# Packed attention and two feed-forward layers on one core: four conversions of w_in2 moved to the end of attention, w_out2's combinations kept as two split parts

## The chip, the cores and the metric

The kernel runs on one core of one Trainium2 chip. The metric is device time in microseconds (us) of one execution. The engines are TensorE (PE in the profile, its weight loads PEld), VectorE (DVE), ScalarE (ACT), GpSimd (POOL) and SyncE (SP). SP issues all DMAs here; sixteen DMA engines move the data.

## What is computed

The reference, cut to what matters:

```python
def sm_attn(qq, kk, vv):                       # softmax attention
    s = scale * qq @ kk.T; a = exp(s - max(s)); a = a / (sum(a) + 1e-09)
    return a @ vv
p_packed = sm_attn(p, k, v)                    # 8 batches, 8 heads, 32 packed queries, 576 keys, width 64
out = sm_attn(q, p_packed, p_packed)           # 576 queries over the 32 packed rows
x = out.transpose(0, 2, 1, 3).reshape(4608, 512)
h = x @ w_in                                   # first layer, 512 -> 2048
y = maximum(0.01 * h, h) @ w_out               # 2048 -> 512
h = y @ w_in2                                  # second layer, 512 -> 2048
result = (h * 1 / (1 + exp(-1.702 * h))) @ w_out2
```

The four weight matrices arrive as 64-bit floats, as pairs of 32-bit words, and have to be converted on the chip.

## The kernel before

**Stages.** There are four, one after the other on PE: attention with the first product h1 (`l1`, line 338; 256 steps, 32 for each of 8 batches), the product y (line 650, 6 blocks of 768 tokens), the product h of the second layer (line 684, 48 units) and the last product, called sum or d (line 762, 6 blocks).

**Seven products.** y, h and sum use Strassen's scheme: in a 2x2 splitting seven products of combinations stand in the place of eight. A y or sum block has 56 steps (7 products of 8 inner tiles), and the whole stage y 336; a unit of h has 7 steps, the whole stage 336 too.

**Split operands.** Each 32-bit operand is split into a high part (a ScalarE cast to fp32r) and a low part (a VectorE subtraction of the high part from the original, line 107); PE multiplies high by high, high by low and low by high. In y the moving operand `ba` is split so from `br`, two steps ahead (line 492 and line 107); `da` and `dr` are the same in the last stage. VectorE also forms the sums and differences of the `br` tiles (lines 480 to 486).

**Conversions.** `combine` converts one of 16 pieces of a weight matrix and forms its seven combinations: three loads into `raw` (512 KB in all), two ScalarE operations (lines 121 and 122, into the tiles `b` and `v`), a bit mask and a shift on VectorE (125 and 128), an integer addition on GpSimd (129), four VectorE subtractions (144 to 148), and a store of `b[:, 1:8]` to a scratch tensor in DRAM (448 KB). The tiles `raw`, `b` and `v` exist once each, so a conversion waits for the one before to be through with them. For w_out1 (`wo1`) the result is split on the spot: a cast and a subtraction into a tile `hl` of their own (lines 155 and 157), and two stores. For w_in2 (`wi2`) and w_out2 (`wo2`) the combinations are stored unsplit. Those of w_in2 are split as they are used in h (`wj`); those of w_out2 in `weights`: each of 14 weight tiles is loaded into its low half, and two times a ScalarE cast (line 459) and a VectorE subtraction follow, each on half of the tile, five tiles (`EARLY`) in stage h, nine in the first block of the last stage.

**What sets the order.** Everything is written out by hand: `at(step, ...)` puts a piece of work into an agenda, `side(step)` issues it between the matmuls of the steps, and each engine runs its instructions in that order. `pieces` spreads one conversion over steps; `combined(what, first, late)` starts one at each step s of `first` and does the rest at s+late, s+late+1, s+late+2, s+late+5 and so on. Before the change the w_in2 conversions begin in y at steps 26 and 44 of block 0, at 1, 19 and 38 of blocks 1 to 4, and at 1 and 19 of block 5; those of w_out2 in h every 15 steps, with late 10. In attention there are those of w_out1, every 11 steps from step 30 to 195, with late 8.

**Around the border of attention and y.** From step 212 on SP also loads the first weights of y (`wo_early`), and at step 248 the twelve first `br` tiles; it stores two h1 tiles of g after every four steps (line 347). The weights that are not early (`wo`) take memory that attention's tiles give back when their last stores have landed.

Of the kernel before, what the change touches and what calls it, by code (L numbers as in the profile page):

```python
# [9 lines left out]
F32 = mybir.dt.float32  # L10
# [11 lines left out]
P = 128  # L22
# [24 lines left out]
def packed_attention_moe_moe_kernel(tc, qT, kT, vm, vt, pT, w_in1, w_out1, w_in2, w_out2, out):  # L47
# [8 lines left out]
    wi2c, wo2c = (tc.dram_tile([NJ, P, 7, 256], F32, name=f"{n}_scratch") for n in ("wi2", "wo2"))  # L56
    wo1c = tc.dram_tile([NJ, P, 2, 7, 256], F32, name="wo1_scratch")
# [22 lines left out]
    with ExitStack() as ctx:  # L80
# [51 lines left out]
        def combine(name, source, scratch):  # L132
# [16 lines left out]
            if scratch is not wo1c:  # L149
                yield  # L150
                nc.sync.dma_start(place(name, scratch), b[:, 1:8])
                return
            yield
            h = pools["px"].tile([P, 2, 7, P], F32R, tag="hl", name=f"hl_{name}")
            nc.scalar.copy(h[:, 0], b[:, 1:8])
            yield
            nc.vector.tensor_sub(h[:, 1], b[:, 1:8], h[:, 0].bitcast(F32))
            yield
            for x in range(2):
                nc.sync.dma_start(place(name, scratch)[:, x], h[:, x].bitcast(F32))  # L160
# [5 lines left out]
        def combined(what, first, late):  # L166

            view, to = {"wo1": (w_out1_v, wo1c), "wi2": (w_in2_v, wi2c), "wo2": (w_out2_v, wo2c)}[what]
            for n, s in enumerate(first):
                j, u = divmod(n, 2)  # L170
                src = view[:, :, u, :, j, :] if what == "wi2" else view[:, :, j, :, u, :]
                pieces(combine(f"{what}_{j}_{u}", src, to), (s, *(s + late + k for k in (0, 1, 2, 5, 6, 7, 8, 9))))
# [258 lines left out]
        combined("wo1", range(30, 30 + 16 * 11, 11), 8)  # L431

# [3 lines left out]
        def weights(first, halves, i, fq, home, scratch, nm):  # L436
# [3 lines left out]
            def load():  # L440
                if n < EARLY:
                    if n == 0:
                        early[nm] = pools["A"].tile([P, 7 * 4 * HB], F32R, tag="A", name=f"{nm}_early")
                    t = early[nm][:, 2048 * n:2048 * n + 2048].rearrange("p (s f w) -> p s f w", s=2, f=4)
                else:
                    t = pools[home].tile([P, 2, 4, 256], F32R, tag=f"w{n}", name=f"{nm}_{p}_{fq}")
                wt[p, fq] = t
                for x in range(2):
                    if scratch is wo1c:
                        nc.sync.dma_start(t[:, x].bitcast(F32), scratch[4 * fq:4 * fq + 4, :, x, COMBO[p], :].rearrange("f p w -> p f w"))  # L450
                    elif x:
                        nc.sync.dma_start(t[:, 1].bitcast(F32), scratch[4 * fq:4 * fq + 4, :, COMBO[p], :].rearrange("f p w -> p f w"))
            at(first, load)
            if scratch is wo1c:
                return

            def half(k):
                hi, lo = (wt[p, fq][:, s, 2 * k:2 * k + 2, :] for s in range(2))
                nc.scalar.copy(hi, lo.bitcast(F32))
                return lo, lo.bitcast(F32), hi.bitcast(F32)  # L460
            for k, step in enumerate(halves):
                split(step, lambda k=k: half(k))
# [70 lines left out]
        def later_weights(home, scratch, nm):  # L533
            for n in range(EARLY, 14):
                i, fq = divmod(n, 2)
                weights(max(8 * (i - 2) + 2 * fq - 8, -2), (8 * i - 6 + 2 * fq, 8 * i - 5 + 2 * fq), i, fq, home(n), scratch, nm)


        for k in range(EARLY):
            s = 32 * (B - 2) + 20 + 8 * k  # L540
            weights(s, (s + 5, s + 7), k // 2, k % 2, None, wo1c, "wo1")
# [94 lines left out]
        combined("wi2", [26, 44] + [56 * blk + k for blk in range(1, 5) for k in (1, 19, 38)] + [281, 299], 14)  # L636
# [91 lines left out]
        for k in range(EARLY):  # L728
            s = 7 * (4 * NJ + 2 * k + 2)
            weights(s, (s + 8, s + 12), k // 2, k % 2, None, wo2c, "wo2")  # L730
# [81 lines left out]
```

## Time and profile before

| | us |
|---|---|
| median of 3 runs | 1481.79 (1481.16 to 1482.88) |
| the profiled execution, its own time | 1488.2 |
| its span, first to last instruction | 1486.4 |
| PE busy / PEld busy | 1417.2 / 1322.9 |
| VectorE busy | 1107.5 |
| ScalarE busy | 836.2 |
| GpSimd busy | 100.4 |
| data moved by DMA | 317.42 MB, 214 GB/s on average |

PE is busy for 95% of the span; the other engines are read where PE has to wait. A time in the rows below counts from the start of the span. A bracket behind a row is the idle time of its engine just before it, and what ended it.

### The profile page before, as it was taken

How to read it: one execution, taken by the hardware profiler on the slowest of the kernel's cores; microseconds unless marked ns; L12 is line 12 of the kernel's file. 1: busy time of each engine (PE TensorE's matmuls, PEld its weight loads, DVE VectorE, ACT ScalarE, POOL GpSimd, SP SyncE). 2: the span in 40 equal slices, each digit the busy share in tenths (PEclk: the TensorE clock that was granted, in tenths of full speed). 3: DMA queues.
4: the chain of work that ended last, by engine and by line, in shares of the span. 5: the costliest groups of instructions: out<-in, count | busy, mean ns of one | idle time of the engine just before them, and what ended most of it. 6: DMA issues, size and time to landing. Idle time of an engine off the chain costs nothing.

```text
span 1486.4 us, 27714 instructions
## 1 busy us (share of the span) xinstructions
PE 1417.2 (95%) x10400; PEld 1322.9 (89%) x10400; DVE 1107.5 (75%) x2068; ACT 836.2 (56%) x1791; POOL 100.4 (7%) x71
## 2 busy tenths in 40 slices
PE   6789999999979999999889999999999999999998
PEld 4567777778979999999789999999999999999998
DVE  5667777762859888888987887877648877777776
ACT  3656666665435545555656766666645655445443
POOL 1311110100001010110100010000000000000000
PEclk8889999999989999999999999999999999999999
DMA  9459999969993655635357786786768524515421
GB/s 365 159 194 318 308 325 307 335 212 337 325 301 118 212 187 164 223 105 197 120 184 249 250 282 238 244 276 204 242 216 276 170 88 148 181 54 170 129 85 43
DMA packets 228773, 317.42 MB, mean 214 GB/s; under 512 B 12576, under 2 KB 188704, under 8 KB 228640
## 3 DMA queue, kind: packets, MB, share of 16 engines
q1 hardware_dynamic: 228640, 315.67, 63.9%
q8 instruction: 81, 1.33, 0.4%
q14 instruction: 52, 0.43, 0.1%
HBM read 191.89 MB, written 123.73 MB: 212 GB/s over the span
## 4 chain that ended last, share of the span: by engine, by line
PE 71%; DVE 17%; issue 4%; DMA 3%; ACT 2%; POOL 2%; SPq 1%; DVEq 0%; ACTq 0%; POOLq 0%
PE sum L762 23%; PE h L684 20%; PE y L650 14%; PE h L338 10%; DVE ba L107 3%; PE m L218 2%; POOL b_wi L129 1%; PE pp L273 1%; PE s L218 1%; DVE m L327 1%; DVE br L482 1%; DVE br L484 1%; DVE wj L107 1%; DVE ya L107 1%; DVE da L107 1%
## 5 line engine op out<-in xcount | busy, mean ns | idle before, releaser
L684 PE MATMUL h<-ya,wj 128*128 128x384 f32 x2016 | 357.7, 338 | 6.7 <-DVE uv L692 2.4
L684 PEld LDWEIGHTS h<-ya,wj 128*128 128x128 f32 x2016 | 352.5, 189 | 11.7 <-DVE uv L692 4.1
L338 PEld LDWEIGHTS h<-a,m 128*128 128x128 f32 x1536 | 215.7, 195 | 53.7 <-ACT g L343 22.1
L650 PE MATMUL y<-ba,wo 128*128 128x384 f32 x1296 | 238.1, 341 | 19.6 <-DVE ba L107 10.9
L650 PEld LDWEIGHTS y<-ba,wo 128*128 128x128 f32 x1296 | 225.6, 189 | 31.2 <-DVE ba L107 22.4
L492 ACT CAST ba<-br 128x384 fp32r<-128x384 f32 x336 | 164.5, 513 | 149.7 <-PE y L650 89.8
L338 PE MATMUL h<-a,m 128*128 128x288 f32 x1536 | 239.5, 309 | 9.3 <-ACT a L315 3.5
L492 ACT CAST da<-dr 128x384 fp32r<-128x384 f32 x336 | 166.3, 514 | 145.2 <-PE sum L762 105.4
L762 PE MATMUL sum<-wo,da 128*128 128x256 f32 x1944 | 232.4, 281 | 1.6 <-DVE da L107 1.4
L762 PEld LDWEIGHTS sum<-wo,da 128*128 128x128 f32 x1944 | 230.2, 188 | 3.2 <-DVE da L107 3.2
L107 DVE TENSOR_TENSOR da<-dr,da 128x384 fp32r<-128x384 f32 x336 | 172.8, 554 | 40.5 <-ACT da L492 40.4
L107 DVE TENSOR_TENSOR ba<-br,ba 128x384 fp32r<-128x384 f32 x336 | 175.7, 556 | 25.5 <-ACT ba L492 25.5
L343 ACT ACTIVATE g<-h 128x288 f32<-128x288 f32 x256 | 105.2, 416 | 99.7 <-PE h L338 98.0
L762 PE MATMUL sum<-wo_early,da 128*128 128x256 f32 x1080 | 132.4, 285 | 1.7 <-ACT da L492 1.6
L762 PEld LDWEIGHTS sum<-wo_early,da 128*128 128x128 f32 x1080 | 131.5, 193 | 2.2 <-ACT da L492 1.9
L650 PE MATMUL y<-ba,wo_early 128*128 128x384 f32 x720 | 128.2, 340 | 2.3 <-ACT ba L492 2.2
L650 PEld LDWEIGHTS y<-ba,wo_early 128*128 128x128 f32 x720 | 126.4, 190 | 3.3 <-ACT ba L492 2.4
L327 DVE TENSOR_TENSOR m<-m,m 128x512 fp32r<-128x512 f32 x64 | 43.0, 684 | 54.6 <-ACT m L325 54.2
L129 POOL TENSOR_TENSOR b_wo<-v_wo,b_wo 128x512 int32<-128x512 int32 x32 | 42.5, 1330 | 485.5 <-DVE v_wo L128 367.6
L677 ACT ACTIVATE g<-cc 128x384 f32<-128x384 f32 x96 | 50.4, 525 | 31.6 <-DVE cc L700 27.1
L107 DVE TENSOR_TENSOR wj<-wjs,wj 128x512 fp32r<-128x512 f32 x88 | 55.8, 647 | 9.7 <-ACT wj L626 9.7
L692 DVE TENSOR_TENSOR uv<-uv,h 128x384 f32<-128x384 f32 x48 | 26.5, 553 | 46.5 <-PE h L684 39.9
(114 smaller groups left out, 1372.1 us busy)
## 6 DMA issues: line engine op xcount, KB each, us to landing
g_scratch<-g SPq DMA_DIRECT2D x64, 576.0 KB, 5.3
br<-g_scratch SPq DMA_DIRECT2D x96, 384.0 KB, 7.0
g_scratch<-g SPq DMA_DIRECT2D x96, 384.0 KB, 5.4
dr<-g_scratch SPq DMA_DIRECT2D x96, 384.0 KB, 4.3
wjs<-wi_scratch SPq DMA_DIRECT2D x22, 896.0 KB, 5.8
wo_scratch<-hl_wo SPq DMA_DIRECT2D x32, 448.0 KB, 6.0
wo<-wo_scratch SPq DMA_DIRECT2D x27, 512.0 KB, 8.9
k<-in_kT_dram SPq DMA_DIRECT2D x16, 576.0 KB, 6.3
```

Of the source, the lines that this page charges most:

```text
L107: at(step + 1, lambda: nc.vector.tensor_sub(*rest))
L129: nc.gpsimd.tensor_tensor(d, v.bitcast(I32), d, op=ALU.add)
L218: nc.tensor.matmul(tiles[par][32 * i:32 * i + 32, :n], lhsT=lhsT(r, i, par), rhs=rhs(r, i), start=True, stop=True)
L327: nc.vector.tensor_sub(m[:, 1, par, :], t[par], m[:, 0, par, :].bitcast(F32))
L338: nc.tensor.matmul(t[:, :TH], lhsT=m[:, ws, par, o:o + P], rhs=a[:, xs, par, :], start=(k == 0), stop=(k == 5))
L343: nc.scalar.activation(g1t[g][:, f % 2, hf * TH:hf * TH + TH], t[:, :TH], AF.Prelu, alpha=0.01)
L492: nc.scalar.copy(t[:, 0, :], src)
L650: nc.tensor.matmul(acc[BANK[p]][:, c, :HB], lhsT=w[:, ws, P * c:P * c + P], rhs=x[:, xs, :], start=(p in OPENS and f + m == 0), stop=(f == ...
L677: nc.scalar.activation(g[f][:, HB * i:HB * i + HB], src, AF.Gelu_apprx_sigmoid)
L684: nc.tensor.matmul(b, lhsT=w[:, ws, c, P * kk:P * kk + P], rhs=x[:, xs, kk, :], start=(p in OPENS and kk + s == 0), stop=(kk + s == 3), sk ...
L692: nc.vector.tensor_add(v, v, b)
L762: nc.tensor.matmul(b, lhsT=x[:, xs, P * c:P * c + P], rhs=w[:, ws, :], start=(p in OPENS and f == 0 and m == 0 and c != 1), stop=(f == NJ ...
```

## The change

Three things. The first four conversions of w_in2 (pieces 0_0, 0_1, 1_0, 1_1) are begun at attention's steps 206, 217, 228 and 239, behind the last of w_out1; y keeps those of blocks 1 to 4 at the same steps, where the pieces are now 2_0 to 7_1, and blocks 0 and 5 have none. Conversions of w_out2 end as those of w_out1 do, with a cast into a tile `hi` and a subtraction, which is made in place in `b`, and two stores of 448 KB each. And the weights of the last stage are loaded as two parts, without casts and subtractions.

```diff
-    wi2c, wo2c = (tc.dram_tile([NJ, P, 7, 256], F32, ...) for n in ("wi2", "wo2"))
-    wo1c = tc.dram_tile([NJ, P, 2, 7, 256], F32, name="wo1_scratch")
+    wi2c = tc.dram_tile([NJ, P, 7, 256], F32, name="wi2_scratch")
+    wo1c, wo2c = (tc.dram_tile([NJ, P, 2, 7, 256], F32, ...) for n in ("wo1", "wo2"))
...
-            if scratch is not wo1c:
+            if scratch is wi2c:
                 yield
                 nc.sync.dma_start(place(name, scratch), b[:, 1:8])
                 return
             yield
-            h = pools["px"].tile([P, 2, 7, P], F32R, tag="hl", name=f"hl_{name}")
-            nc.scalar.copy(h[:, 0], b[:, 1:8])
-            yield
-            nc.vector.tensor_sub(h[:, 1], b[:, 1:8], h[:, 0].bitcast(F32))
-            yield
-            for x in range(2):
-                nc.sync.dma_start(place(name, scratch)[:, x], h[:, x].bitcast(F32))
+            lo = b[:, 1:8].bitcast(F32R)
+            if scratch is wo1c:
+                h = pools["px"].tile([P, 2, 7, P], F32R, tag="hl", name=f"hl_{name}")
+                h, lo = h[:, 0], h[:, 1]
+            else:
+                h = pools["c1"].tile([P, 7, P], F32R, tag="hi", name=f"hi_{name}")
+            nc.scalar.copy(h, b[:, 1:8])
+            yield
+            nc.vector.tensor_sub(lo, b[:, 1:8], h.bitcast(F32))
+            yield
+            for x, t in enumerate((h.bitcast(F32), lo.bitcast(F32))):
+                nc.sync.dma_start(place(name, scratch)[:, x], t)
...
         combined("wo1", range(30, 30 + 16 * 11, 11), 8)
+        combined("wi2", range(206, 206 + 4 * 11, 11), 8)
...
-                    if scratch is wo1c:
-                        nc.sync.dma_start(t[:, x]..., scratch[4 * fq:4 * fq + 4, :, x, COMBO[p], :]...)
-                    elif x:
-                        nc.sync.dma_start(t[:, 1]..., scratch[4 * fq:4 * fq + 4, :, COMBO[p], :]...)
+                    nc.sync.dma_start(t[:, x]..., scratch[4 * fq:4 * fq + 4, :, x, COMBO[p], :]...)
             at(first, load)
-            if scratch is wo1c:
-                return
-            def half(k):
-                hi, lo = (wt[p, fq][:, s, 2 * k:2 * k + 2, :] for s in range(2))
-                nc.scalar.copy(hi, lo.bitcast(F32))
-                return lo, lo.bitcast(F32), hi.bitcast(F32)
-            for k, step in enumerate(halves):
-                split(step, lambda k=k: half(k))
...
-        combined("wi2", [26, 44] + [56 * blk + k for blk in range(1, 5) for k in (1, 19, 38)] + [281, 299], 14)
+        combined("wi2", [56 * blk + k for blk in range(1, 5) for k in (1, 19, 38)], 14, 4)
```

The last argument of `combined` is new: the number of the first piece. Line numbers of the changed file differ by a few.

SP's order at the end of attention, before (`g_7_...` are h1 tiles of the last batch, `br_...` the first data of y):

```order
L347 DMA g_scratch<-g_7_4_4354 128x2x576
L450 DMA wo_early<-wo_scratch 128x4x256 x2
L347 DMA g_scratch<-g_7_6_4400 128x2x576
L347 DMA g_scratch<-g_7_8_4439 128x2x576
L450 DMA wo_early<-wo_scratch 128x4x256 x2
L347 DMA g_scratch<-g_7_10_4485 128x2x576
L471 DMA br_000_4521<-g_scratch 128x2x384
```

And the same place in the changed kernel:

```order
L352 DMA g_scratch<-g_7_4_4389 128x2x576
L455 DMA wo_early<-wo_scratch 128x4x256 x2
L352 DMA g_scratch<-g_7_6_4436 128x2x576
L138 DMA raw_wi_1_1_4475<-in_w_in_dram 128x256 x2
L139 DMA raw_wi_1_1_4475<-in_w_in_dram 128x2x256
L352 DMA g_scratch<-g_7_8_4486 128x2x576
L151 DMA wi_scratch<-b_wi_1_0_4440 896x1x128
L455 DMA wo_early<-wo_scratch 128x4x256 x2
L352 DMA g_scratch<-g_7_10_4537 128x2x576
L465 DMA br_000_4577<-g_scratch 128x2x384
```

Loads and stores of the four conversions now stand between the g stores and the early weights, ahead of the first `br` load; the store of 1_1 comes after the `br` loads.

ScalarE's order in y's block 0, before (the casts of `ba` for product 4, with the conversion between them; in the changed kernel the two rows of `b_wi` and `v_wi` are not there):

```order
L492 CAST ba_4_2_5063<-br_111_4539 128x384
L517 COPY c_0_5071<-y_4624 128x768
L492 CAST ba_4_3_5075<-br_111_4539 128x384
L121 ACTIVATE b_wi_0_0_5077<-raw_wi_0_0_4932 128x512
L122 ACTIVATE v_wi_0_0_5078<-raw_wi_0_0_4932 128x512
L492 CAST ba_4_4_5090<-br_112_4541 128x384
L492 CAST ba_4_5_5103<-br_112_4541 128x384
```

So the casts of `ba_4_4` and behind stand behind the two operations on `raw_wi_0_0` before, and directly behind `ba_4_3` after.

SP's order in stage h around the store of conversion 1_0 of w_out2, before:

```order
L138 DMA raw_wo_1_1_8940<-in_w_out_dram 128x256 x2
L139 DMA raw_wo_1_1_8940<-in_w_out_dram 128x2x256
L151 DMA wo_scratch<-b_wo_1_0_8880 896x1x128
L710 DMA g_scratch<-g_6_0_8861 128x768
L710 DMA g_scratch<-g_6_1_8862 128x768
L710 DMA g_scratch<-g_7_0_8947 128x768
```

And in the changed kernel:

```order
L138 DMA raw_wo_1_1_8948<-in_w_out_dram 128x256 x2
L139 DMA raw_wo_1_1_8948<-in_w_out_dram 128x2x256
L704 DMA g_scratch<-g_6_0_8869 128x768
L704 DMA g_scratch<-g_6_1_8870 128x768
L165 DMA wo_scratch<-hi_wo_1_0_8975 128x7x128
L165 DMA wo_scratch<-b_wo_1_0_8888 128x7x128
L704 DMA g_scratch<-g_7_0_8955 128x768
```

The store of `b` has become two, of `hi` and of `b`, and they stand two steps later, here behind the two g stores of unit 6. On ScalarE the next conversion's L121, which writes `b`, keeps its place.

## Rows read from the trace of the kernel before

**Rows 1.** Windows: length, busy PE, PEld, DVE, ACT, POOL, clock, DMA share, GB/s.

```profile
326.00:359.00 33.00, 32.28 (x269) 27.87 (x268) 11.80 (x21) 18.44 (x45) 0.00 (x0) 1.00 0.96 310
368.00:370.00 2.00, 2.00 (x8) 2.00 (x7) 0.62 (x2) 1.49 (x4) 0.00 (x0) 0.50 1.07 375
381.00:420.00 39.00, 34.38 (x197) 33.73 (x195) 26.17 (x44) 15.38 (x31) 0.00 (x0) 0.99 1.04 340
424.00:426.00 2.00, 1.29 (x4) 0.89 (x5) 2.00 (x4) 1.35 (x4) 0.13 (x1) 0.50 0.94 322
751.00:870.00 119.00, 115.44 (x643) 113.46 (x643) 93.12 (x181) 76.17 (x165) 8.03 (x6) 0.99 0.73 253
870.00:1000.00 130.00, 127.97 (x727) 126.48 (x726) 104.92 (x209) 83.88 (x186) 10.63 (x8) 1.00 0.75 251
1117.00:1178.00 61.00, 59.36 (x479) 58.55 (x480) 55.70 (x95) 38.20 (x79) 0.00 (x0) 0.97 0.74 249
```

**Rows 2.** Timeline of PE: starts of y's blocks 0, 1, 2, 5, and h.

```profile
367.05 0.44 PE L650 MATMUL y<-ba,wo_early 128*128 128x384 f32 x1 [2.17 <-ACT ba L492]
...
439.50 21.42 PE L650 MATMUL y<-ba,wo_early 128*128 128x384 f32 x120
501.26 20.97 PE L650 MATMUL y<-ba,wo_early 128*128 128x384 f32 x120
...
684.04 20.97 PE L650 MATMUL y<-ba,wo_early 128*128 128x384 f32 x120
751.16 4.15 PE L684 MATMUL h<-ya,wj 128*128 128x384 f32 x23
```

**Rows 3.** Timeline of all engines in y's block 0.

```profile
412.63 2.54 SPq L138 DMA_DIRECT2D raw_wi<-in_w_in_dram  x2
...
422.09 0.66 ACT L121 ACTIVATE b_wi<-raw_wi 128x512 int32<-128x512 uint32 x1 [9.50 <-DMA raw_wi<-in_w_in_dram]
...
423.75 0.69 PE L650 MATMUL y<-ba,wo 128*128 128x384 f32 x1 [8.25 <-ACT ba L492]
```

**Rows 4.** Timeline of all engines where attention ends and y begins.

```profile
359.42 10.59 SPq L471 DMA_DIRECT2D br<-g_scratch  x12
...
366.49 2.62 ACT L492 CAST ba<-br 128x384 fp32r<-128x384 f32 x5 [1.16 <-DMA br<-g_scratch]
```

**Rows 5.** Waits of PEld, 690 to 760: total us, times, longest.

```profile
PEld y L650 <- DVE ba L107: 9.2, 13, 1.7
```

**Rows 6.** Groups by form, DVE: conversions in y, split in attention, last stage's halves.

```profile
L125 DVE TENSOR_SCALAR raw_wi<-raw_wi 128x512 uint32<-128x512 uint32 x16 | 6.8, 425 | 12.4 <-ACT v_wi L122 11.3 <-DMA br<-g_scratch 1.1
...
L128 DVE SCALAR_TENSOR_TENSOR v_wi<-v_wi,raw_wi 128x512 uint32<-128x512 uint32 x16 | 11.0, 685 | 0.0
L144 DVE TENSOR_TENSOR b_wi<-b_wi 128x128 f32<-128x128 f32 x16 | 4.6, 286 | 7.1 <-POOL b_wi L129 7.1
...
L157 DVE TENSOR_TENSOR hl_wo<-b_wo,hl_wo 128x896 fp32r<-128x896 f32 x16 | 17.3, 1082 | 6.7 <-ACT hl_wo L155 4.3 <-DMA raw_wo<-in_w_out_dram 1.1 <-DMA g_scratch<-g 1.1
...
L107 DVE TENSOR_TENSOR wo<-wo 128x512 fp32r<-128x512 f32 x18 | 12.5, 694 | 0.0
```

**Rows 7.** DMA issues, 751 to 1117: count, KB each, median us to landing.

```profile
wo_scratch<-b_wo SPq DMA_DIRECT2D x16, 448.0 KB, 4.6
```

**Rows 8.** DMA issues of the whole span (all of these in attention).

```profile
wo_scratch<-hl_wo SPq DMA_DIRECT2D x32, 448.0 KB, 6.0
```

**Rows 9.** Waits of ACT in stage h.

```profile
ACT b_wo L121 <- DMA wo_scratch<-b_wo: 2.0, 3, 1.0
```

**Rows 10.** Timeline of all engines in stage h, 915 to 931.

```profile
920.25 0.67 ACT L121 ACTIVATE b_wo<-raw_wo 128x512 int32<-128x512 uint32 x1 [1.83 <-issue]
...
921.50 0.43 DVE L125 TENSOR_SCALAR raw_wo<-raw_wo 128x512 uint32<-128x512 uint32 x1 [2.44 <-ACT v_wo L122]
...
928.87 2.37 PE L684 MATMUL h<-ya,wj 128*128 128x384 f32 x12 [1.46 <-DVE uv L692]
```

**Rows 11.** Waits of PEld in the last stage, 1115 to 1185.

```profile
PEld sum L762 <- DVE da L107: 2.3, 4, 0.8
```

More of the change, by code (lines that the diff above doesn't have):

```diff
@@ L55, in packed_attention_moe_moe_kernel @@
     g2 = tc.dram_tile([NF, P, NT], F32, name="g2_scratch")
-    wi2c, wo2c = (tc.dram_tile([NJ, P, 7, 256], F32, name=f"{n}_scratch") for n in ("wi2", "wo2"))
-    wo1c = tc.dram_tile([NJ, P, 2, 7, 256], F32, name="wo1_scratch")
+    wi2c = tc.dram_tile([NJ, P, 7, 256], F32, name="wi2_scratch")
+    wo1c, wo2c = (tc.dram_tile([NJ, P, 2, 7, 256], F32, name=f"{n}_scratch") for n in ("wo1", "wo2"))
     w_in1_v = w_in1.bitcast(U32).rearrange("(k p) w -> p k w", p=P)
@@ L164, in place, with combined @@
             return scratch[int(j)][..., P * int(u):P * int(u) + P]
-        def combined(what, first, late):
+        def combined(what, first, late, start=0):
             view, to = {"wo1": (w_out1_v, wo1c), "wi2": (w_in2_v, wi2c), "wo2": (w_out2_v, wo2c)}[what]
-            for n, s in enumerate(first):
+            for n, s in enumerate(first, start):
                 j, u = divmod(n, 2)
@@ L431, in packed_attention_moe_moe_kernel, with weights @@
         combined("wo1", range(30, 30 + 16 * 11, 11), 8)
+        combined("wi2", range(206, 206 + 4 * 11, 11), 8)
         steps = [(blk, p, f) for blk in range(NBK) for p in PRODUCTS for f in range(NJ)]
         wt, raws, ga, outs, early = {}, {}, {}, {}, {}
-        def weights(first, halves, i, fq, home, scratch, nm):
+        def weights(first, i, fq, home, scratch, nm):
             p, n = PRODUCTS[i], 2 * i + fq
@@ L448, in load @@
                 for x in range(2):
-                    if scratch is wo1c:
-                        nc.sync.dma_start(t[:, x].bitcast(F32), scratch[4 * fq:4 * fq + 4, :, x, COMBO[p], :].rearrange("f p w -> p f w"))
-                    elif x:
-                        nc.sync.dma_start(t[:, 1].bitcast(F32), scratch[4 * fq:4 * fq + 4, :, COMBO[p], :].rearrange("f p w -> p f w"))
+                    nc.sync.dma_start(t[:, x].bitcast(F32), scratch[4 * fq:4 * fq + 4, :, x, COMBO[p], :].rearrange("f p w -> p f w"))
             at(first, load)
-            if scratch is wo1c:
-                return
-            def half(k):
-                hi, lo = (wt[p, fq][:, s, 2 * k:2 * k + 2, :] for s in range(2))
-                nc.scalar.copy(hi, lo.bitcast(F32))
-                return lo, lo.bitcast(F32), hi.bitcast(F32)
-            for k, step in enumerate(halves):
-                split(step, lambda k=k: half(k))
         def load_raw(blk, i, h, fp, nm, g):
@@ L535, in later_weights @@
                 i, fq = divmod(n, 2)
-                weights(max(8 * (i - 2) + 2 * fq - 8, -2), (8 * i - 6 + 2 * fq, 8 * i - 5 + 2 * fq), i, fq, home(n), scratch, nm)
+                weights(max(8 * (i - 2) + 2 * fq - 8, -2), i, fq, home(n), scratch, nm)
         for k in range(EARLY):
             s = 32 * (B - 2) + 20 + 8 * k
-            weights(s, (s + 5, s + 7), k // 2, k % 2, None, wo1c, "wo1")
+            weights(s, k // 2, k % 2, None, wo1c, "wo1")
         order = {b: [(f, hf) for f in range(NF) for hf in range(2)] for b in range(B)}
@@ L729, in packed_attention_moe_moe_kernel @@
             s = 7 * (4 * NJ + 2 * k + 2)
-            weights(s, (s + 8, s + 12), k // 2, k % 2, None, wo2c, "wo2")
+            weights(s, k // 2, k % 2, None, wo2c, "wo2")
         at(7 * (6 * NJ - 3), *(lambda fp=fp: load_raw(0, 1, 0, fp, "d", g2) for fp in range(4)))
```

## The prediction

> **What bounds the kernel now.** I read the span from the side of TensorE: it is busy 1417 of 1486.4 us, so an edit off TensorE pays only where TensorE waits for what the edit touches. The windows come first [rows 1], then the timeline of PE in the y stage, cut where a block begins [rows 2]. The six blocks begin at 367.05, 439.50, 501.26, 684.04 (three blocks later) and end at 751.16. So block 0 takes 72.4 us, block 1 61.8, blocks 2 to 4 together 182.8 or 60.9 each, and block 5 67.1. All six have the same matmuls; blocks 0 and 5 are long by 11.5 and 6.2 us. The engines' timeline shows why for block 0 [rows 3]: ScalarE stands 9.50 us before its L121 of conversion wi2_0_0 until that conversion's raw data land, because SP issued the loads only at 412.63. The casts of ba for the next steps stand behind L121 on ScalarE, so PE gets nothing for 8.25 us; then it runs at a granted clock of 0.50 [rows 1], the lower level of 1.2 GHz. Block 5 is another matter: PE waits there 13 times, 9.2 us, for VectorE's low parts of ba [rows 5]. Attention's last stretch, 326 to 359, is the reverse: PE 32.28 of 33 us, VectorE 11.80, GpSimd nothing, but the DMA engines at a share of 0.96 [rows 1].
>
> **Part 1, conversions out of block 0.** One conversion issues three loads (512 KB), two ScalarE operations, six on VectorE, one on GpSimd, one store (448 KB). Without wi2_0_0 in block 0, ScalarE's next cast is that of the following step, whose source was loaded before the stage began. I take the block to shrink to the length of blocks 2 to 4: -11.5 us. That holds the 8.25 us, the part of the half clock behind it, and the start. What is late next are the weights: SP is behind in this block, with DMA at 340 GB/s and a share over 1 [rows 1], and part 2 pushes all of it later. If a weight load becomes late, 1 to 3 us of the 11.5 stay.
>
> **Part 2, the same conversions at the end of attention.** Their engine work is hidden there: VectorE is idle 21 of 33 us, ScalarE 14.6, GpSimd 33 [rows 1]; no other GpSimd work is passed, and SP's four issues per conversion stand between g stores that SP waits for anyway. Their transfers are not hidden. Three raw loads and three stores (3 x 512 KB and 3 x 448 KB, 2.95 MB) are issued on SP ahead of the twelve br loads of 359.42; the first wi2 load falls earlier, the last store behind them. PE's first y matmul waits for the first br already: the ACT cast at 366.49 is released by that DMA [rows 4]. At the 310 GB/s of this stretch, 2.95 MB take 9.5 us; the 4% that the engines stand idle absorb 1.3, so the start slips by 8 us at most. If instead 340 GB/s could have been had all along, 33 us hide 33 x 30/340 = 2.9 us of 8.7, and it slips by 5.8. The lower bound is 2, if most of the bytes go before the queue fills at 326. A gain is excluded, since the br loads stand behind these bytes. I take 6, by the second, since 340 GB/s is what a queue that was never empty moved from 381 on, plus 1 us because wi2_1_1's L121 may hold the last g activations and so let PE stand before y starts: the clock was at 0.50 after the 2.17 us wait there [rows 1, 4], and after the 8.25 us wait too. Part 2 costs +7 (2 to 11). The Trainium skill, TensorE: Matmul & The Clock Gate, section "Part 1: The HAM clock gate", says that the throttled clock is the default and that idleness brings it back. By that rule alone a longer stop at the start of y would cost some 2 us more than I take; the rows agree that idling lowers the clock, not yet how much more here.
>
> **Part 3, conversions out of block 5.** VectorE is the late engine there. Two conversions are 2 x (0.43 + 0.69 + 4 x 0.29) = 4.5 us on it [rows 6], L144 waits for GpSimd besides (7.1 us in 16 conversions, 0.9 for two), together 5.4 of the 6.2 us by which the block is long. The sum takes -5 (bounds -2.5, if half of it was in gaps, and -6.2, the whole surplus).
>
> **Part 4, w_out2 in two parts, stage h.** Gone from h are ten halves (early weights), gone from the last stage eighteen: 28 x 0.69 = 19.4 us on VectorE and as many casts on ScalarE. Added in h are 16 casts and 16 subtractions of 128x896; the subtraction takes 1.08 us in attention [rows 6], so 17.3 us on VectorE, most of them before 1000, where it is busy 93.1 of 119 and 104.9 of 130 us [rows 1]. That fits in, and so do 16 more stores of 448 KB where the DMA share is 0.73 to 0.75. What need not fit is the wait: the low part is now made in place in tile b, so b is free for the next conversion's L121 only when its store has landed. The store's place in the order moves from step s+17 to s+19 while the next L121 stays at s+25, and it is the second of a pair. A step is (1117 - 751) / 336 = 1.09 us [rows 1]. So the way from store to L121 shrinks from 8.7 to 6.5 us, while the landing grows: 4.6 us median for a single store, 6.0 for each of a pair in attention [rows 7, 8]. The margin loses 2.2 + 1.4 = 3.6 us. It was thin before: ScalarE waits there already, three times for 2.0 us and once 1.83 us [rows 9, 10]. If the other eleven margins lie evenly between 0 and 6 us, about ten of fifteen waits come out at 2 to 3 us, 25 us on ScalarE, and behind L121 stand the copies of u and v and the g activations, on VectorE L125 and all behind it. PE does not feel each: a PSUM bank is written again three steps later, so 3 x 1.09 less the wait and the length of a copy leaves some 2.4 us where nothing else is late (an estimate from these rows). Where casts of ya and wj are due, it does: the one wait of 1.83 us became 2.44 us on VectorE and 1.46 us on PE [rows 10]. I let a third through: +8. Ends: 0, if ScalarE's idle third takes it all, and +20, if nearly every wait comes through; below nothing it can hardly go, as the ten halves leave a stretch behind the last conversions, where the two windows before already have PE busy for all but 2 or 3% [rows 1].
>
> **Part 5, the last stage.** Without its eighteen halves VectorE has 12.5 us less in the first block, where it was busy 55.7 of 61 us and PE waited 2.3 us for it [rows 1, 6, 11]: -1.5 (0 to -2.5). Nine more loads of 512 KB lift the block from 249 to about 326 GB/s, under the 340 that the like block of y sustains [rows 1]; with SP on time they cost nothing, otherwise a microsecond or two.
>
> **Sum.** -11.5 + 7 - 5 + 8 - 1.5 = -3.0 us. The profiled execution took 1488.2 us for a span of 1486.4; it lies 6.4 us over the median of the runs, 1481.8. The difference is carried over as it is: 1481.8 - 3 = 1478.8, say 1479.
>
> **Rivals.** (a) The waits for b's store stay inside ScalarE's idle time. For it: ScalarE is idle a third of h, and the three old waits of 2.0 us together are each under what a bank's three steps allow. Against it: the fourth old wait reached PE [rows 10]. Part 4 then costs about 1: -10 us, 1472. (b) Slower: the in-place low part. One mechanism, in h: L121 waits for the second store of the pair in nearly every conversion, VectorE's L125 waits with it, and since VectorE has little room left (80% busy, now 86%), each delay is still there when the next comes. At +18 for part 4 the sum is +7: 1489. It decides from the point where more than 14 us of the estimated 25 reach PE. (c) Block 0's stall comes back at the end of attention: wi2_1_1's raw data land late in the full queue, ScalarE stands at its L121 with the last g activations behind, and weights in y's first block become late as well. Part 2 then costs 12 instead of 7 and part 1 gives 1 less, sum +3: about 1484.5. (d) That the change doesn't do what it says is excluded by the order of instructions.
>
> **How the numbers follow.** Forecast 1479 (its own range 1474 to 1484): 0.40. (a) 0.27, (b) 0.22, (c) 0.11. The range of 1468 to 1490 takes in (a) and (b) with the bounds of parts 2 and 4 and leaves out less than 0.2. A measurement of this kernel can tell about 0.2%, 3 us, from no change, so the lines are 1478.8 and 1484.8. Faster: (a) and 0.16 of the forecast, 0.43. Same: 0.22 of the forecast and most of (c), 0.29. Slower: (b), the rest of (c) and 0.02 of the forecast, 0.28.
>
> **What would show it.** Right: block 0 near 61 us and no wait of ScalarE for raw_wi in it; the first br landing 5 to 8 us later against the end of attention's matmuls; block 5 near 62; in h, ten or so waits of L121 for the store, 20 to 30 us together, and h longer by about 8; the last stage's first block shorter by 1 to 2. Wrong: part 2 if y starts on time; part 1 if PE waits in block 0 for weights; part 4 if the waits of L121 stay under 8 us, or if h is no longer in spite of them.

## The result and the profile after

The changed kernel takes 1503.55 us in the median of its runs (1501.42 to 1505.17), where before takes 1482.34 beside it: a ratio of 1.0123 (95% interval 1.0092 to 1.0154). It is slower by 1.2%, 21 us; 1479 was forecast, and 1490 was the upper end.

In the traces the span grows by 16.2 us, from 1486.4 to 1502.6. The other 5 us are the scatter of executions: before's profiled one lies 6 us over its median, the one of after 1 us. The beginnings of the stages and blocks on PE, the answer to [rows 2] (timeline of PE of the changed kernel, with the two first blocks of the last stage from a closer look):

```profile
382.81 3.99 PE L644 MATMUL y<-ba,wo_early 128*128 128x384 f32 x19 [0.90 <-ACT ba L486]
...
442.90 20.97 PE L644 MATMUL y<-ba,wo_early 128*128 128x384 f32 x120
...
503.79 20.97 PE L644 MATMUL y<-ba,wo_early 128*128 128x384 f32 x120
...
686.64 20.97 PE L644 MATMUL y<-ba,wo_early 128*128 128x384 f32 x120
...
749.16 3.11 PE L678 MATMUL h<-ya,wj 128*128 128x384 f32 x17
...
1136.26 1.93 PE L756 MATMUL sum<-wo_early,da 128*128 128x256 f32 x11 [1.60 <-ACT da L486]
...
1196.99 2.20 PE L756 MATMUL sum<-wo_early,da 128*128 128x256 f32 x17
```

Differences of such beginnings give the account. The last batch of attention is counted from its first l1 matmul (335.5 in before, 335.0 after). Before's last stage begins at 1117.2 and its second block at 1181.0.

| us | before | after | difference | forecast |
|---|---|---|---|---|
| up to attention's last batch | 335.5 | 335.0 | -0.5 | 0 |
| attention's last batch, to y | 31.6 | 47.8 | +16.3 | +7 |
| y, block 0 | 72.4 | 60.1 | -12.3 | -11.5 |
| y, block 1 | 61.8 | 60.9 | -0.9 | 0 |
| y, block 5 | 67.1 | 62.5 | -4.6 | -5 |
| h | 366.0 | 387.1 | +21.1 | +8 |
| last stage, first block | 63.8 | 60.7 | -3.1 | -1.5 |

The gains came as they were worked out. The two losses are 37 us instead of 15.

**Attention's end.** The waits of ScalarE from 326 to 385 (total us, times, longest), and the place of the longest in the timeline of all engines:

```profile
ACT b_wi L121 <- DMA wi_scratch<-b_wi: 8.8, 2, 6.5
ACT b_wi L121 <- issue: 2.7, 1, 2.7
```

```profile
336.01 0.81 SPq L151 DMA_DIRECT2D wi_scratch<-b_wi  x1
...
344.79 0.66 ACT L121 ACTIVATE b_wi<-raw_wi 128x512 int32<-128x512 uint32 x1 [6.54 <-DMA wi_scratch<-b_wi]
...
345.89 0.71 ACT L348 ACTIVATE g<-h 128x288 f32<-128x288 f32 x2
...
346.35 5.79 PEld L343 LDWEIGHTS h<-a,m 128*128 128x128 f32 x30 [5.19 <-ACT g L348]
346.35 5.89 PE L343 MATMUL h<-a,m 128*128 128x288 f32 x29 [4.96 <-ACT g L348]
```

The store of 0_0's `b` is issued at 336.01. 0_1's L121, which writes the same tile, is in order four steps behind it, and stands until the store has landed. The g activations that free h1's banks stand behind L121, and PE stops. 1_0 and 1_1 do the same, shorter: for 1_0 the profile names no releaser ("issue"), but the store of 0_1's `b` landed at 359.54 and L121 began at 359.69, while its raw data were there at 352.24. The clock falls behind the stop (window of 340 to 350; columns as in [rows 1]):

```profile
340.00:350.00 10.00, 5.04 (x26) 4.81 (x25) 3.42 (x8) 3.85 (x9) 1.28 (x1) 0.68 0.71 237
```

The stops are only half of the loss. The windows of attention's last batch, before and then after:

```profile
335.50:367.05 31.55, 29.38 (x242) 26.14 (x240) 4.17 (x7) 16.56 (x41) 0.00 (x0) 1.00 0.97 329
```

```profile
334.97:382.81 47.84, 36.71 (x242) 31.49 (x241) 11.97 (x29) 19.34 (x47) 3.84 (x3) 0.82 0.85 282
```

PE does the same 242 matmuls; it is idle for 11.1 us instead of 2.2, and busy for 36.7 instead of 29.4, at a mean granted clock of 0.82 instead of 1.00. So 9.0 of the 16.3 us are stops, and 7.3 are matmuls at the lower clock behind them. How much of the second comes scatters: in six traces of kernels whose code is the same up to there (the first part alone and five that differ only in h) the batch lasts 44.5 to 48.1 us.

The first `br` was issued at 373.47, but by 382.25, when the first cast of `ba` ran, attention's own matmuls had only just ended: at the border PE waits 0.90 us, less than the 2.17 of [rows 2].

**Stage h.** The page's row of h's matmuls, of the changed kernel and then of before (busy, mean ns | idle before them):

```profile
L678 PE MATMUL h<-ya,wj 128*128 128x384 f32 x2016 | 364.6, 341 | 20.9 <-ACT uv L682 14.8
```

```profile
L684 PE MATMUL h<-ya,wj 128*128 128x384 f32 x2016 | 357.7, 338 | 6.7 <-DVE uv L692 2.4
```

Of the 21.1 us, 14.2 are idle time (20.9 less 6.7), most of it waiting for ScalarE's copies of u, and 6.9 are the same matmuls taking longer. About half of these go with the clock: the granted clock is 0.57 from 886 to 890, from 934 to 938 and from 1019 to 1023, before only from 777 to 781, and 4 us at 0.57 are 1.7 us lost. The other half isn't traced to a cause. Groups by line in h (busy, mean ns | idle just before, and what ended it), the answer to [rows 9]:

```profile
L162 DVE TENSOR_TENSOR b_wo<-b_wo,hi_wo 128x896 fp32r<-128x896 f32 x16 | 17.4, 1088 | 4.1 <-ACT hi_wo L160 3.9
...
L160 ACT CAST hi_wo<-b_wo 128x896 fp32r<-128x896 f32 x16 | 15.1, 942 | 16.4 <-issue 11.4 <-DVE b_wo L148 4.9
...
L121 ACT ACTIVATE b_wo<-raw_wo 128x512 int32<-128x512 uint32 x16 | 10.7, 668 | 24.8 <-DMA wo_scratch<-b_wo 22.8 <-DMA g_scratch<-g 2.1
```

L121 stands 24.8 us (25 were estimated); the new cast L160 stands 16.4 us for VectorE. (The profile names VectorE for 4.9 of them and no releaser for 11.4, but there too the cast begins less than 0.1 us behind the end of L148.) One of L121's long waits, in the timeline of all engines:

```profile
916.59 2.14 SPq L573 DMA_DIRECT2D yq<-y_scratch  x4
...
919.69 1.71 SPq L165 DMA_DIRECT2D wo_scratch<-b_wo  x1
...
929.24 0.66 ACT L121 ACTIVATE b_wo<-raw_wo 128x512 int32<-128x512 uint32 x1 [3.85 <-DMA wo_scratch<-b_wo]
...
934.01 2.29 PE L678 MATMUL h<-ya,wj 128*128 128x384 f32 x6 [2.20 <-ACT uv L682]
```

The store lies behind four loads of y and lands 9.5 us after its issue, where the median is 5.9; ScalarE waits 3.85 us, and 2.6 us later PE stops for 2.20. Then the granted clock is 0.57 in the mean, mostly the lower of its two levels, 1.2 GHz (window of 934 to 938):

```profile
934.00:938.00 4.00, 3.99 (x13) 3.68 (x13) 3.90 (x9) 1.79 (x4) 0.07 (x1) 0.57 0.87 290
```

A longer wait does not always cost more. The longest of all, from the same timeline at 970 to 1002, is followed by a shorter stop, and from 982 to 986 the granted clock is 1.00:

```profile
980.21 0.67 ACT L121 ACTIVATE b_wo<-raw_wo 128x512 int32<-128x512 uint32 x1 [5.19 <-DMA wo_scratch<-b_wo]
...
982.68 8.85 PE L678 MATMUL h<-ya,wj 128*128 128x384 f32 x48 [1.88 <-ACT uv L682]
```

Which stores land late can be read from SP's order. In h of the changed kernel eight of the sixteen stores of `b` have another load or store, besides the first of their pair, issued at most 2.7 us ahead of them; they landed in 6.8 to 9.5 us. The other eight landed in 3.1 to 4.9. Each of the late ones, and none of the others, is followed by a wait at L121, of 2.1 to 5.2 us.

**The last stage.** PEld's waits for VectorE's `da` in 1130 to 1200 fell from the 2.3 us of [rows 11] to:

```profile
PEld sum L756 <- DVE da L107: 0.5, 2, 0.3
```

The window of its first block, the answer to the last of [rows 1]: the added loads take the DMA engines to 340 GB/s, and PE is busy 60.61 of 61 us. The granted clock of the block is 1.00, where it was 0.97 [rows 1].

```profile
1136.00:1197.00 61.00, 60.61 (x505) 60.20 (x506) 45.91 (x78) 31.22 (x63) 0.00 (x0) 1.00 1.03 340
```

### The profile page after: what moved, and what is told of

The parts are those of the page before. It is cut to its first block, busy times and chain, and to the rows that moved or that the text cites. A ratio compares the mean times of both kernels' runs of the same rounds, so it can differ in the third digit from the quotient of the medians.

```text
span 1502.6 us, 27772 instructions
## 1 busy us (share of the span) xinstructions
PE 1423.7 (95%) x10400; PEld 1323.6 (88%) x10400; DVE 1106.6 (74%) x2056; ACT 834.0 (55%) x1779; POOL 95.2 (6%) x71
## 5 line engine op out<-in xcount | busy, mean ns | idle before, releaser
L678 PE MATMUL h<-ya,wj 128*128 128x384 f32 x2016 | 364.6, 341 | 20.9 <-ACT uv L682 14.8
L343 PEld LDWEIGHTS h<-a,m 128*128 128x128 f32 x1536 | 217.2, 196 | 67.1 <-ACT g L348 30.8
L644 PE MATMUL y<-ba,wo 128*128 128x384 f32 x1296 | 234.2, 338 | 7.1 <-DVE ba L107 6.6
L644 PEld LDWEIGHTS y<-ba,wo 128*128 128x128 f32 x1296 | 223.7, 188 | 16.8 <-DVE ba L107 16.2
L223 PE MATMUL m<-w,ppk 64*32 64x512 f32 x512 | 51.1, 644 | 9.1 <-POOL w L129 9.0
```

Of the source, the lines that this page charges most:

```text
L223: nc.tensor.matmul(tiles[par][32 * i:32 * i + 32, :n], lhsT=lhsT(r, i, par), rhs=rhs(r, i), start=True, stop=True)
L343: nc.tensor.matmul(t[:, :TH], lhsT=m[:, ws, par, o:o + P], rhs=a[:, xs, par, :], start=(k == 0), stop=(k == 5))
L644: nc.tensor.matmul(acc[BANK[p]][:, c, :HB], lhsT=w[:, ws, P * c:P * c + P], rhs=x[:, xs, :], start=(p in OPENS and f + m == 0), stop=(f == ...
L678: nc.tensor.matmul(b, lhsT=w[:, ws, c, P * kk:P * kk + P], rhs=x[:, xs, kk, :], start=(p in OPENS and kk + s == 0), stop=(kk + s == 3), sk ...
```

## The experiments

Two theories were set against each other. The theory of the wait: what was lost is ScalarE standing at L121, since `b` is one tile and free only when its store has landed. The theory of the work: what was lost is the bytes (2.95 MB at the end of attention, 16 more stores in h) and VectorE's subtractions. In these runs before takes 1487 to 1489 us, so they are told by their ratio to it and by the lengths of stages in their traces (PE's timeline, as above).

**The parts alone.** The first kernel is before with only the move of w_in2; the second is after with the move taken back:

```diff
-        combined("wi2", range(206, 206 + 4 * 11, 11), 8)
-        combined("wi2", [56 * blk + k for blk in range(1, 5) for k in (1, 19, 38)], 14, 4)
+        combined("wi2", [26, 44] + [56 * blk + k ...] + [281, 299], 14)
```

> The kernel before with the first part alone: the four w_in2 conversions at the end of attention, w_out2 unsplit as before. In the changed kernel y begins 15.7 us later than before and h begins 2.0 us earlier, so y's blocks 0 and 5 gave back 12.3 and 4.6 us. If the parts are independent, this kernel repeats that up to the start of h (y from about 383, block 0 near 60 us, block 5 near 62.5), h lasts 366 us as before and the last stage's first block 63.8: total 1480, between 1477 and 1484. If the loss in h comes from the moved conversions (other places of raw or b, other times of the first weights), h is long here too, 380 or more, and the total is near 1495.

> The changed kernel with the w_in2 conversions put back into y's blocks 0 and 5: the second part alone. Attention and y as before (y from 367, block 0 72 us, h from 751). If the waits for b's store in h are the loss, h lasts 384 to 390 instead of 366 us, ScalarE's L121 waits 20 to 30 us in it, the last stage's first block is about 3 us shorter, and the total is 1498 to 1504. If h was long only because the conversions in attention shifted it against the loads, h is 370 or less and the total under 1485.

The move alone: 0.9975 (0.9962 to 0.9987), 1484.5 us; attention's last batch lasts 44.5 us (it begins at 333.3 and y at 377.8), blocks 0 and 5 last 60.3 and 62.5, h 367.1. The split alone: 1.0129 (1.0109 to 1.0149), 1505.0 us; attention and y as in before, h lasts 385.8, the last stage's first block 60.4. The product of the two ratios is 1.0104, within the interval of the whole. So the two parts add up as if they were independent, and h's loss belongs to the split. The waits of the split alone in h:

```profile
ACT b_wo L121 <- DMA wo_scratch<-b_wo: 15.6, 7, 3.4
...
ACT hi_wo L160 <- issue: 11.4, 10, 2.2
ACT b_wo L121 <- DMA g_scratch<-g: 5.7, 1, 5.7
```

**More room before the next L121, one place each.** In attention 0_0 and 1_0 write into a tile of their own; in h the conversions begin every 17 steps:

```diff
-            b = conv.tile([P, 8, P], F32, tag="b", ...)
+            if name in ("wi2_0_0", "wi2_1_0"):      # the tile hl of w_out1's conversions
+                b = pools["px"].tile([P, 2, 7, P], F32R, tag="hl", ...)...
```

```diff
-        combined("wo2", range(3, 3 + 16 * 15, 15), 10)
+        combined("wo2", range(3, 3 + 16 * 17, 17), 10)
...
-            s = 7 * (4 * NJ + 2 * k + 2)
+            s = 7 * (4 * NJ + 2 * k + 2) + 35
```

> The changed kernel, in which w_in2 conversions 0_0 and 1_0 write into the tile that w_out1's conversions have left (hl), so that no conversion at the end of attention waits for the store of the one before. The same bytes, at the same places of SP's order. Theory of the wait: the 6.5, 2.6 and 2.5 us that ScalarE stands at L121 there go, and the g activations behind it are on time; what is left of the 15.7 us is the bytes, 5 to 8 us; y begins at 372 to 376, the total is 1492 to 1497. Theory of the bytes: the transfers are late whatever waits for them, y begins at 380 or later, total 1500 or more.

> The changed kernel with the w_out2 conversions begun every 17 steps of h instead of every 15 (and the early weights of the last stage loaded 35 steps later, since the last conversion ends later). Between the store of b and the next L121 lie 8 steps again, as before the change. Theory of the wait: L121 waits under 8 us in h instead of 26, h lasts 367 to 373 us instead of 387, total 1484 to 1490. Theory of the work (17 us of subtractions on VectorE, 16 more stores): the work is the same, h stays at 380 or more, total 1497 or more.

The second tile: 1.0060 (1.0043 to 1.0077), y begins at 375.3. That is where the theory of the wait put it, but not all as thought: L121 of 0_0 now waits for w_out1's last store out of hl, so that the batch itself begins 5 us later (340.1). From there to y it lasts 35.2 us, 3.7 more than before; but this loss ahead of it belongs to the second tile, so the run doesn't tell by itself what the bytes cost:

```profile
ACT b_wi L121 <- DMA wo_scratch<-hl_wo: 4.5, 1, 4.5
```

Every 17 steps: 1.0027 (1.0015 to 1.0039). h lasts 375.3 us. That is 12 less than after, but 2 to 8 more than expected. L121's waits fell only to 10 us, L160's stayed, and near the end a conversion now meets loads of `wj`:

```profile
ACT hi_wo L160 <- issue: 11.7, 9, 3.0
ACT b_wo L121 <- DMA wo_scratch<-b_wo: 10.0, 7, 3.1
ACT hi_wo L160 <- DVE b_wo L148: 6.8, 4, 2.4
ACT wj L620 <- DMA wjs<-wi_scratch: 5.3, 2, 3.9
```

**Attention with half the bytes, and with all of them earlier.** Both start from before, without the split:

```diff
+        combined("wi2", (206, 222), 8)
...
+        combined("wi2", [56 * blk + k for blk in range(1, 5) for k in (1, 19, 38)] + [281, 299], 14, 2)
```

```diff
-        combined("wo1", range(30, 30 + 16 * 11, 11), 8)
+        combined("wo1", range(30, 30 + 16 * 10, 10), 8)
+        combined("wi2", range(191, 191 + 4 * 11, 11), 8)    # 0_1 and 1_1 in hl
```

> The kernel before with only the two conversions of y's block 0 (0_0 and 0_1) moved to the end of attention, begun at steps 206 and 222, so that 0_1 writes b nine steps after 0_0's store was issued; block 5 keeps its two, w_out2 stays unsplit. The bytes alone, half of those of the whole move, and no wait for b. Theory of the wait: ScalarE does not stand at L121, and y begins 2 to 4 us later than before (half of the 3.6 us by which attention's last batch was longer with four conversions and a second b, and up to half of my 8). Block 0 lasts 60.5 us, block 5 67, h 366: the total is 8 to 10 us under before. Theory of the bytes: y begins 7 us later or more, and the total is 5 us under before or less.

> The kernel before with the four conversions moved, w_out2 unsplit, and no wait for b's store: w_out1's conversions begin every 10 steps instead of every 11, the four of w_in2 from step 191 on, and 0_1 and 1_1 write into the tile hl, so that each b or hl is written again 15 steps after its store. Most of the bytes also go before the queue is full at the end. Theory of the wait: no L121 waits over 1 us, y begins 1 to 4 us later than before, blocks 0 and 5 give back 12 and 4.6 us as before, total 12 to 16 us under before. If the bytes are the cost, y begins 7 us or more later and the total is 10 us under before or less. Against both: w_out1's conversions, packed closer, may themselves make attention longer.

Two moved: 0.9914 (0.9895 to 0.9934), 1475.5 us, the best kernel of the study that computes the whole, faster than before and after. y begins at 367.3, block 0 lasts 60.8 us, block 5 67.4 as it did, h 365.8. From the start of the batch, two conversions cost 2.4 us. The saving of 13 us is a few more than expected; in the trace, 2 of them are the batch beginning earlier (333.4). The second kernel: 0.9935 (0.9913 to 0.9956). Within the last batch it loses 2.9 us to before, and no L121 waits for `b` there (one waits 2.1 us, for raw data); but it begins the batch at 344.3, and in all it is 9 us under before, not 12 to 16. The last objection in the expectation holds: w_out1's conversions every 10 steps make attention longer by 9 us before the place in question.

**h with the end of the conversion drawn together.** At 15 steps, and with everything mended:

```diff
-... (s, *(s + late + k for k in (0, 1, 2, 5, 6, 7, 8, 9)))
+... (s, *(s + late + k for k in ((0, 1, 2, 5, 6, 6, 7, 7) if what == "wo2" else ...)))
```

> The changed kernel with the last pieces of a w_out2 conversion drawn together: the cast into hi in the step of the last two subtractions, the in-place low part and both stores in the next, two steps earlier than in the changed kernel. The spacing stays 15 steps, so between the store of b and the next L121 lie 8 steps instead of 6, as in the kernel begun every 17 steps, by another way. Theory of the wait: L121 waits 8 to 12 us instead of 26, h lasts 372 to 378 us instead of 387, total 10 to 14 us under the changed kernel, 4 to 9 over before. If the spacing of 17 steps helped because the work was spread thinner (or because the early weights were loaded later), h stays at 380 or more here.

> Everything together: the changed kernel with w_out1 every 10 steps, w_in2's four from 191 with 0_1 and 1_1 in hl, w_out2 every 17 steps (early weights 35 steps later) and its last pieces drawn together, so that 10 steps lie between the store of b and the next L121 in h. If the waits add up as they did apart, y begins 1 to 4 us later than before, h lasts 367 to 371 us, the last stage's first block is 3 us shorter: total 11 to 17 us under before. If the work of the split in h costs something without the waits, h is 373 or more and this kernel is slower than the same without the split.

Both kernels missed what was expected: 1.0085 (1.0054 to 1.0116) and 1.0050 (1.0032 to 1.0069). h lasts 385.5 and 385.6 us, as long as with the split alone, though L121 waits only 7.4 and 6.0 us (in the second kernel for raw data, not for `b`). The waits of `wo_tight`, and those of `both_mended` (its L164 is L160, L152 is L148):

```profile
ACT hi_wo L160 <- issue: 25.0, 11, 4.3
...
ACT b_wo L121 <- DMA wo_scratch<-b_wo: 7.4, 3, 3.3
...
ACT hi_wo L160 <- DVE b_wo L148: 6.0, 3, 2.9
```

```profile
ACT hi_wo L164 <- DVE b_wo L152: 18.5, 10, 3.4
...
ACT g L675 <- DMA g_scratch<-g: 13.3, 8, 4.8
...
ACT hi_wo L164 <- issue: 11.0, 5, 3.0
```

The cast, put into the step of VectorE's last two subtractions, waits 31.0 and 29.5 us for them (16.4 in after), up to 4.3 at a time. In the second kernel the g activations besides wait 13.3 us for stores of g, 2.8 in after. One wait was exchanged for another on the same engine. This left the theory open: either ScalarE's stops are the loss, whatever they wait for, or the added work is.

**h without the wait, at the same work.** The low part goes into `hi` in place of `b`, so that both stores read `hi` and the high part of w_out2 is left out; then, besides, the cast comes two steps later:

```diff
-                h = pools["c1"].tile([P, 7, P], F32R, tag="hi", name=f"hi_{name}")
+                h = lo = pools["c1"].tile([P, 7, P], F32R, tag="hi", name=f"hi_{name}")
```

```diff
-... k in (0, 1, 2, 5, 6, 7, 8, 9)
+... k in ((0, 1, 2, 5, 6, 9, 10, 11) if what == "wo2" else (0, 1, 2, 5, 6, 7, 8, 9))
```

> The changed kernel, in which the low part of w_out2 is subtracted into hi instead of b (and so both stored parts are the low one: the high part of w_out2 is left out of the result). The same instructions, bytes and places; only b is free after the subtraction and no longer after the store's landing. Theory of the store: L121 waits under 4 us in h instead of 26, h lasts 366 to 372 us, total 1483 to 1490 where the changed kernel takes some 1507 on a chip on which before takes 1489. Rival, from the kernels with 8 and 10 steps of margin that waited only 6 to 8 us at L121 and still had an h of 385 us: ScalarE's new cast L160, which waits for VectorE's last two subtractions (16 us of waits in the changed kernel), does the same harm; then h stays at 376 or more.

> The same kernel with, besides, the cast into hi two steps later behind the last two subtractions (its subtraction and stores follow two steps later as well; the high part of w_out2 is left out as there). With b free early, the two steps cost no margin. If both waits of ScalarE are the loss, that for the store at L121 and that for VectorE at L160, both are under 5 us in sum and h lasts 365 to 369 us, 3 to 10 us less than with b free alone. If VectorE's added work (17.3 us of subtractions in a stage where it is busy 80%) is the loss, h stays where it was with b free alone, or above 376.

The first: 0.9989 (0.9976 to 1.0002), h lasts 368.8 us instead of 387.1. The second: 0.9985 (0.9974 to 0.9996), h 367.4. All instructions, bytes and places are those of after in the first kernel, and 18.3 of the 21.1 us are gone. This settles h: the loss is the wait for the store and what comes with it. The page's row of h's matmuls in the first kernel says in what form it went:

```profile
L678 PE MATMUL h<-ya,wj 128*128 128x384 f32 x2016 | 357.1, 337 | 10.1 <-ACT uv L682 3.4
```

Against after, 10.8 us of idle time (20.9 less 10.1) and 7.5 us of busy time (364.6 less 357.1) are gone. In the second kernel 1.4 us are left over before (367.4 against 366.0). That is the new work (subtractions, casts, stores) less the ten halves that the change took out of h, and within the scatter: in five traces without the split h lasts 365.4 to 367.2 us. The rest of L160's waits, in the first:

```profile
ACT hi_wo L160 <- issue: 9.6, 10, 1.9
```

With three more, put down to other releasers, there are thirteen waits, of up to 1.9 us and 12.4 us together, and h is 2.8 us over before. In `wo_tight` L160's waits reach 4.3 us and come to 31.0, and h is as long as with the waits for the store. Length and sum differ together here, so these runs don't tell which of the two decides.

**Attention without the wait, at the same bytes.** On top of the last kernel, three stores read another tile, so that three pieces of w_in2 are left out as well:

```diff
-                nc.sync.dma_start(place(name, scratch), b[:, 1:8])
+                kept = w1[:, 0, :7 * P]... if name in ("wi2_0_0", "wi2_0_1", "wi2_1_0") else b[:, 1:8]
+                nc.sync.dma_start(place(name, scratch), kept)
```

> The kernel with b free and a late cast in h, in which besides the stores of w_in2's 0_0, 0_1 and 1_0 at the end of attention read the tile w1 in place of b (the high part of w_out2 and these three pieces of w_in2 are left out of the result). Stores of the same size at the same places of SP's order; no L121 at the end of attention can wait for one of them. Theory of the wait: the first stop of ScalarE, 6.5 us for 0_1's L121, and the one of 1_0 go, attention's last batch (from its first l1 step to y) lasts 34 to 36 us, where it lasts 31.6 before, 47.8 in the changed kernel and 35 with a second b; block 0 to 5 as in the changed kernel, h 367: the total is 11 to 14 us under the kernel with b free and a late cast, 12 to 16 under before. Theory of the bytes: the queue delays the g stores and br loads anyway, the last batch lasts 42 us or more, and the total is at most 6 us under that kernel. This kernel is also the price of both parts of the change if no wait for b's store came with them.

0.9902 (0.9879 to 0.9925), 1473.4 us. The last batch of attention lasts 36.0 us (336.0 to 371.9), where it lasts 31.6 before and 47.8 after. The bytes cost 4.4 us, the wait 11.8 with the lower clock behind it (8.5 to 12 by the scatter of the batch). The stores' own place on SP is no rival: in after SP stands only 0.5 us for `b` there. Of the waits of ScalarE's L121 there, one is left, the one for raw data that rival (c) had named:

```profile
ACT b_wi L121 <- DMA raw_wi<-in_w_in_dram: 2.5, 1, 2.5
```

**Better still?** Two moved, and the other fourteen conversions spread evenly, to free block 5:

```diff
+        combined("wi2", range(50, 50 + 14 * 16, 16), 14, 2)
```

> The kernel before with w_in2's first two conversions at the end of attention (steps 206 and 222, as in the kernel with two moved) and the other fourteen every 16 steps from step 50 of y to step 258, so that block 5 has only the end of the last one; w_out2 unsplit. Block 0 and the start of y as with two moved (367, 60.8 us), blocks 1 to 4 at 61 us with 3.5 conversions each instead of 3, block 5 at 62.5 to 63.5 instead of 67.4, h 366: total 4 us under the kernel with two moved, 17 under before. Against it: if the blocks between have no room for a fourth conversion (VectorE, or the queue), they grow by 1 us or more each and nothing is won.

0.9949 (0.9931 to 0.9966): faster than before, but not than two moved alone (0.9914; the intervals just touch, and the trace is 3.9 us longer). Block 5 lasts 62.5 us as hoped, but the four blocks between last 62.4 to 64.0 instead of 60.9. PEld's waits for VectorE in blocks 1 to 4, first here, then with two moved alone:

```profile
PEld y L651 <- DVE ba L107: 20.1, 35, 1.4
```

```profile
PEld y L651 <- DVE ba L107: 11.2, 20, 0.8
```

The objection held: the blocks with four conversions last 63.8 and 64.0 us. But those with three, as before, last 62.4 at the new steps, so their places count too.

## Why the prediction was wrong, point by point

- **Part 1** (-11.5): right, -12.3, and no weight load came late; block 1 gave 0.9 more, which the sum did not have. Two moved alone gives the same 11.6 of block 0.
- **Part 2** (+7, 2 to 11): wrong, +16.3. The term for the bytes, 6, was not too low: without the wait they cost 4.4 us. The path that it took for them, y waiting for the first `br`, was not the one: at the border PE waits less than before. The step that failed is the search for what else could stop ScalarE, for which the sum had 1 us, for 1_1 alone. Rival (c) looked there too, but at the raw data coming late for 1_1. The wait was for `b`, and three conversions stood in it: w_in2's combinations are stored unsplit, straight out of `b`. In the changed kernel's y the next L121 comes 11 steps or more behind the store, at the end of attention four, while the three stores issued there land in 7.8 us in the median. The prediction applied this very reckoning to w_out2 in part 4 and not to w_in2 in part 2. Of the lower clock the sum had no more than a part of that 1 us: the stops are 9.0 us, the slower matmuls behind them 7.3.
- **Part 3** (-5): right, -4.6.
- **Part 4** (+8, 0 to 20): the mechanism was right, the size was not: +21.1, over the upper end. It is the price of rival (b), 18 and more. Its sum of waits was right too, 24.8 us against 25. The step that failed is "I let a third through: +8". PE's idle time grew by 14.2 us: 10.8 of them went when `b` was free early, and 1.7 more when the new cast L160, whose waits part 4 did not have, came later (8.4 us of idle time are left in `b_free_late_cast`). On top come 6.9 us of longer matmuls, about half of them at the lower clock, for which part 4 had no term either. The sizes were not as drawn: not ten waits of 2 to 3 us, all alike, but eight of 2.1 to 5.2, behind the eight stores that landed late (6.8 to 9.5 us, where the reckoning had 6.0). Nor does the allowance of 2.4 us for each decide what comes through: waits of 3.85, 5.19 and 3.27 us were followed by stops of 2.20, 1.88 and 0.99 us, the one of 2.16 by stops of 2.64 and 0.41, and the one of 3.06 by none over 0.3. What decides it for a single wait stays open. The trace agrees in part with what the prediction drew from the Trainium skill (TensorE: Matmul & The Clock Gate, "Part 1: The HAM clock gate"): idleness brings the lower clock back, here 0.57 behind a stop of 2.2 us, but the clock stays at 1.00 behind one of 1.88 us. Rival (b)'s further reason, that VectorE is too full to recover from a delay, wasn't tested: with `b` free early it does the same work in an h of 368.8 us, so its load alone is not the loss, but there are few delays left to recover from.
- **Part 5** (-1.5, 0 to -2.5): right in sign, over its bound, -3.1: the wait for `da` fell from 2.3 to 0.5 us, and no cost of the nine loads more is seen. The rest goes with the granted clock, 1.00 instead of 0.97, a term that part 5 did not have. It does not come each time: in `wo_tight`, with the same last stage, the clock of the block is 0.97 and its length 62.2 us, 1.6 less than before.
- **Rival (a)**, the waits hidden: excluded by h's length. It is where the kernel would be without them, though: `no_store_of_b`, with both waits gone, is 14 us under before.

What stays open: a version of the split that computes the whole and has no wait was not found. A low part in a tile of its own was not tried, and the two ways to give the store more steps exchanged its wait for others.

## What to carry to other kernels

When a conversion is moved or its last step put in place, look first at when its tile may be written again: the steps between the store out of it and the next write, against the slowest landing in that stretch, not the median. A sum of waits on the engine that empties PE's banks is not yet a price: thirteen waits of up to 1.9 us, 12.4 together, went with 2.8 us of h, and freeing `b` early, which took away eight of 2.1 to 5.2 us, 24.8 together, with 18.3. And count the matmuls behind a stop as well as the stop. When a wait is removed by drawing the steps before it together, read the waits of the same engine again before counting the gain.

## What was not expected of the hardware

A stop of PE can cost more than its length: at the end of attention 9.0 us of added idle time came with 7.3 us of slower matmuls, in h 14.2 us with 6.9. It does not each time: the same two stops early in h, of 1.6 and 0.7 us, are followed by a granted clock of 0.57 in before (777 to 781) and of 1.00 in after (775 to 779). Stores of 448 KB in an unsaturated stage (DMA share 0.78 in h of the changed kernel) landed in 3.1 to 9.5 us, late where SP had issued something else just ahead of them. And kernels that are alike up to that point begin attention's last batch between 333.3 and 336.2 us, so a difference of 2 to 3 us in a single pair of traces says nothing.
